# Attention and MLP-mixer on one core: the first k and q by another queue, fewer separate denominators, finer waits

## The chip, the cores and the metric

The kernel runs on one core of one Trainium2 chip. The metric is the device time of one execution in microseconds; of several runs the median is taken. A profile is one execution taken by the hardware profiler; its times are in microseconds from the start of its span.

## What is computed

Eight batches of attention with eight heads of 64 columns over 576 positions, with a decay that depends on a running sum of max(s, 0), and on its output one block of an MLP-mixer:

```python
scores = scale * np.matmul(q, k.transpose(0, 1, 3, 2))
cum = np.cumsum(np.maximum(s, 0.0), axis=-1)
bias = -(cum[:, :, :, None] - cum[:, :, None, :])
scores = np.where(causal, -1000000000.0, scores + np.minimum(bias, 0.0))
attn = np.exp(scores - max); attn = attn / (sum(attn) + 1e-09)
x = heads side by side of np.matmul(attn, v)                 # 8 x 576 x 512
h = np.maximum(xt @ w_tok1, 0.0) @ w_tok2                    # over tokens, 256 wide
u = x + h.transpose(0, 2, 1)
out = u + np.maximum(u @ w_ch1, 0.0) @ w_ch2                 # over channels, 1536 wide
```

## The kernel before

The work is not written in the order in which it runs. Functions (`stage_qk`, `stage_v`, `quad`, `pair`, `tok`, `chan`) hand operations to a planner, `Plan`: each with the engines that may do it, its occupancy and latency on each, what it reads and writes, which buffer it takes and a priority. `Plan.run` walks through time with one clock for each engine and one for the transfers (`dma_free`), always takes the operation that can start first, and among near equals the one of lowest `prio`. The result is one order of instructions for each engine, fixed when the kernel is built. On the chip an engine keeps to that order and waits on semaphores, so an instruction that waits holds up all that stands behind it on its engine. Holes that the plan sees on TensorE in the first 45 us (`WARM`) are filled with products of a zero tile (L1114, "fillers").

Attention goes by batch `b` and by quads of four heads (`h` = 0 and 4). For a quad, k and q are loaded in the layout of 64 rows of 9 x 64 numbers (`load_cast`, L462): by a POOL DMA that casts float32 to bf16 on the way. TensorE transposes the tile (L672), ScalarE or VectorE copies the transposes to kT and qT (L682, L684). A quad holds two pairs, `pair(b, h)` with heads h and h + 2, so that batch 0 has pairs 0, 1, 4 and 5. A pair's scores are computed in two pieces into the two banks of the ring psc (L714); in batch 0 two products first preset the bank with the mask neg (L705), which VectorE builds (L531, L535) from `keep` (POOL, masks.py) and a zeroed tile (ScalarE, L526). ScalarE takes the exponential of a piece of 1024 columns into E (L722).

The decay is folded into v: s is summed along the positions on VectorE (L515, L517, L520), ScalarE takes exp of it into wn (L523), TensorE transposes that (L543), VectorE copies it to wT (L547) and multiplies it into v (`merge_v`, L614). vp has a column more than v, which holds the weight itself (`ones`, L623), so that the product of E and vp gives the denominator in column D. In batch 0 the pairs with h < 5 (0, 1 and 4, `apart`) compute denominators apart: 18 products of one column (L766) into a tile bd as soon as the column is there, and one reciprocal for both heads (L772); their attention products (L784) then leave the column out. These three pairs use banks of the ring pmx, pair 5 one of psc. VectorE or ScalarE normalises into x (L796, L802).

`tok(b)` does the product over tokens (L877 first), and `chan(b)` that over channels: the first product into g in 12 blocks of 128 channels (L995), copied out with max(., 0) (L1002, L1004), and the second product (L1021) in three steps of four blocks (`th`). In the plan, each of the second product's operations reads the whole of g:

```python
gkeys = [(g, cc, a) for cc in range(NCC) for (a, e) in spans]
```

POOL's loads form a chain: each stands after the one before and waits for the eighth before it (`load_op`). The order written at the end of the kernel begins with k and q of quad 0, `ident`, one tile of v, k and q of quad 4, `identf`, `keep`, then the rest of v and the weights. SyncE loads s (L504) and the last tile of v (L592), and later the results.

Of the kernel before, what the change touches and what calls it, by code (L numbers as in the profile page):

```python
# [8 lines left out]
FP32 = mybir.dt.float32  # L9
# [45 lines left out]
class Plan:  # L55
# [50 lines left out]
    def run(self, eps=0.03):  # L106
# [11 lines left out]
        for o in ops:  # L118
            if o.nd == 0:
                for e in o.alts:  # L120
                    cands[e].append(o)
        dma_free = 4.5
        mode = 0
# [19 lines left out]
        while left:  # L143
# [32 lines left out]
            e, est, o = best  # L176
# [191 lines left out]
def kernel(  # L368
# [12 lines left out]
    nc = tc.nc  # L381
# [78 lines left out]
    def load_cast(n, b, h, i, src):  # L460
        def load():
            nc.gpsimd.dma_start(  # L462
                out=n.t[:, i, :, :],
                in_=src[b, h : h + 4, :, :].rearrange("(f e) (p r) d -> (e p) f (r d)", e=2, r=R))
        load_op(load, [(n, i)], 1.6 if i and not (b or h) else 1.45, prio=-1 if b or h else -3)

# [36 lines left out]
    neg = sb("neg", [128, 2, 512], BF16, fast)  # L503
    nc.sync.dma_start(out=s_sb[:, :], in_=s.rearrange("b h s -> (b h) s"))  # L504
    nc.vector.memset(one_sb[:, :], 1.0)
# [7 lines left out]

    P.op({"SP": (0.6, 2.95, lambda: None)}, writes=["s"], prio=-1)
    P.op(dve(576, lambda: nc.vector.tensor_scalar_max(out=s_sb[:, :], in0=s_sb[:, :], scalar1=0.0)),  # L515
# [66 lines left out]
    def stage_v(b, cs=tuple(range(NJ))):  # L582
        if b not in vbuf:
            vbuf[b] = Buf(r_vf), Buf(r_vp[b % 2])
        vf, vp = vbuf[b]
        odd = b % 2
        for c in cs:
            n = min(128, S - c * 128)
            p0 = 64 if odd and n < 128 else 0

            def load_first(c=c, n=n, p0=p0):
                nc.sync.dma_start(out=vf.t[p0 : p0 + n, c, :, :],  # L592
                                  in_=v[b, :, c * 128 : c * 128 + n, :].rearrange("h p d -> p h d"))

            def load(c=c, n=n, p0=p0):
                nc.gpsimd.dma_start(out=vf.t[p0 : p0 + n, c, :, :],  # L596
                                  in_=v[b, :, c * 128 : c * 128 + n, :].rearrange("h p d -> p h d"))
            if b == 0 and c == NJ - 1:
                P.op({"SP": (0.6, 4.6, load_first)}, writes=[(vf, c)], prio=-2)
                continue  # L600
            load_op(load, [(vf, c)], 1.15 * n / 128, 0.92)
        if b:
            merge_v(b, cs)

    def merge_v(b, cs=tuple(range(NJ))):
# [16 lines left out]
        def ones(eng):  # L622
# [3 lines left out]
        P.op({"POOL": (0.5, 0.7, lambda: ones(nc.gpsimd))} if b else {"DVE": (0.25, 0.3, lambda: ones(nc.vector))},  # L626
             reads=["wT"], writes=[(vp, "w")], prio=b * 10 + 5 if b else -1, lock=True)

# [26 lines left out]
    def quad(b, h):  # L655
# [4 lines left out]
        for ti in range(2):  # L660
# [6 lines left out]
            def tr(ti=ti, pv=pv):  # L667
                for r in range(R):
                    for e in range(2):
                        p0 = e * PR  # L670
                        for f in range(2):
                            nc.tensor.transpose(out=pv(e)[f * D : f * D + D, r * PR : (r + 1) * PR],  # L672
                                                in_=nat.t[p0 : p0 + PR, ti, f, r * D : (r + 1) * D],
                                                identity=ident[p0 : p0 + PR, p0 : p0 + PR])
            P.op({"PE": (R * 0.031, R * 0.031 + 0.21, tr)}, reads=[(nat, ti), "ident"] + pads,
                 writes=[(pts[e], e) for e in range(2)], holds=[d[ti] for d in dsts], prio=(np_ - 30 * (b < 1 and h < 1), 2), mode=1)
# [13 lines left out]
    def pair(b, h, kT, qT):  # L690
# [66 lines left out]

        if apart:
            for hh in range(2):
# [14 lines left out]
            P.op({"DVE": (0.2, 0.25, rcp0)}, reads=[(bd, 2 * h), (bd, 2 * h + 1)], writes=[(rc, 0), (rc, 1)], prio=-4)  # L774
        DE = D if apart else D + 1

# [12 lines left out]
        if b == 0:  # L789
            if not apart:  # L790
                def rcp1():
                    nc.vector.reciprocal(out=rc.t[:, :, :], in_=pav2()[:, :, :, D])
                P.op({"DVE": (0.25, 0.3, rcp1)}, reads=[(pas[0], 0), (pas[1], 1)], writes=[(rc, 0), (rc, 1)], prio=-4)
            for hh in range(2):
                def nrm(hh=hh):
                    nc.vector.tensor_tensor(  # L796
                        out=x.t[:, :, (h + 2 * hh) * D : (h + 2 * hh) * D + D], in0=pav(hh)[:, :, 0:D],
                        in1=rc.t[:, hh, :].unsqueeze(2).to_broadcast([128, NJ, D]), op=ALU.mult)
# [181 lines left out]
    def chan(b, u, us, uT):  # L980
# [4 lines left out]
        for (cc, (a, e)) in ([(cc, sp) for hf in range(2) for sp in spans for cc in range(6 * hf, 6 * hf + 6)] if b < 2 else  # L985
                             [(cc, sp) for cc in range(NCC) for sp in spans]):
            if True:
# [5 lines left out]
                def mm(cc=cc, pm=pm, a=a, e=e):  # L993
                    for m in range(NMC):
# [11 lines left out]
                     reads=[(pm, 0)], writes=[(g, cc, a)], prio=0)  # L1006
        gkeys = [(g, cc, a) for cc in range(NCC) for (a, e) in spans]
        for ci, c in enumerate((4, 0, 1, 2, 3) if odd else (0, 1, 2, 3)):
# [7 lines left out]
            for (na, ne) in ([(0, DM)] if whole else [(0, DM // 2), (DM // 2, DM)]):  # L1016
                pm = Buf(r_mx, False)
                for th in range(3):
                    def mm(c=c, pm=pm, th=th, na=na, ne=ne):
                        for cc in range(th * 4, th * 4 + 4):  # L1020
# [18 lines left out]

    stage_qk(0, 0)  # L1040

    def pool_first(occ, fn, key):
        P.op({"POOL": (occ, occ + 0.1, fn)}, writes=[key], prio=-2, after=chain[-1])
# [119 lines left out]
```

## Time and profile before

| | |
|---|---|
| median of 3 runs | 304.81 us (303.45 to 305.19) |
| profiled execution | 303.32 us, its span 301.6 us |
| TensorE busy | 291.0 us, 96% of the span |
| ScalarE, VectorE, POOL busy | 182.5, 174.2, 108.8 us |
| granted TensorE clock, mean | 0.997 |

Rows in order of time give the start, the duration, the engine, the line, the operation with its tiles (out<-in), how many instructions are merged in the row, and in square brackets the idle time before it and what ended it. PE is TensorE, PEld its loading of weights, ACT ScalarE, DVE VectorE, POOL GpSimd, SP SyncE; SPq is SyncE issuing a transfer. Rows of a table by stretches give the stretch, its length, the busy time of PE, PEld, DVE, ACT and POOL, the clock, the share of the transfer engines and GB/s. Rows of transfers give the issuing line, the count, the size of each and the time from issue to landing. TensorE's rows can overlap by some tenths, since its products are pipelined.

### The profile page before, as it was taken

Reading aid. Unit: us, or ns where it says so; the run is one execution under the profiler, and the core shown is the slowest. Engines: PE = TensorE matmul, PEld = TensorE weight load, DVE = VectorE, ACT = ScalarE, POOL = GpSimd, SP = SyncE. Lnnn points to the kernel's source line nnn. Section 1 sums busy time; section 2 is a strip of 40 time slices with the busy share of each in tenths; the row PEclk is TensorE's granted clock in tenths of the full one; section 3 lists DMA queues with packets and bytes.
Section 4 is the critical chain, followed back from the end, with each engine's and each line's share of the span. In section 5 each row is a group of like instructions: output and inputs, shape, how many; then the busy total and the mean of one; then the engine's idle time right before and its main releaser. Section 6 shows DMA issues by size and latency. Waiting matters only on the chain.

```text
span 301.6 us, 8120 instructions
## 1 busy us (share of the span) xinstructions
PE 291.0 (96%) x3431; PEld 169.1 (56%) x3467; DVE 174.2 (58%) x365; ACT 182.5 (61%) x298; POOL 108.8 (36%) x146
## 2 busy tenths in 40 slices
PE   8899999999999999999999999999999999999993
PEld 3468566557754545446764555456764544447542
DVE  6671799597786547665646638776546543430022
ACT  4897994697894587627873277756770367107500
POOL 8885477999491246307440105800000000000000
PEclk9999999999999999999999999999999999999998
DMA  7999999999995593557753461993003310161032
GB/s 133 232 206 206 209 231 232 233 201 282 164 201 103 142 221 59 104 119 149 164 80 73 137 117 23 169 152 125 2 3 70 113 65 0 52 125 51 4 105 77
DMA packets 38348, 38.70 MB, mean 128 GB/s; under 512 B 17600, under 2 KB 31488, under 8 KB 38304
## 3 DMA queue, kind: packets, MB, share of 16 engines
q0 software_dynamic: 17616, 24.84, 45.8%
q1 hardware_dynamic: 20688, 13.26, 16.4%
q8 instruction: 29, 0.48, 0.6%
q14 instruction: 15, 0.12, 0.1%
HBM read 40.65 MB, written 9.44 MB: 166 GB/s over the span
## 4 chain that ended last, share of the span: by engine, by line
PE 83%; DMA 10%; DVE 2%; POOL 2%; issue 2%; ACT 1%; POOLq 0%
PE pmx L995 30%; PE pmx L1021 30%; DMA wc<-in_moe_w_ch_dram 7%; PE pmx L877 5%; PE psc L784 5%; PE psc L714 5%; PE pmx L939 4%; PE psc L672 3%; DMA vf<-in_v_dram 2%; POOL qkn L462 1%; DVE E L739 1%; ACT E L722 1%; POOL vf L596 1%; DVE E L731 0%; DVE ub L946 0%
## 5 line engine op out<-in xcount | busy, mean ns | idle before, releaser
L722 ACT ACTIVATE E<-psc 128x1024 bf16<-128x1024 f32 x64 | 62.1, 1024 | 24.2 <-PE psc L714 23.9
L995 PEld LDWEIGHTS <-wc 128*128 128x128 bf16 x624 | 57.9, 98 | 31.0 <-issue 0.4
L995 PE MATMUL pmx<-uTb,wc 128*128 128x320 bf16 (+2 forms) x384 | 55.9, 299 | 0.0
L1021 PE MATMUL pmx<-wc,gb 128*128 128x512 bf16 (+1 forms) x242 | 54.0, 369 | 0.8 <-issue 0.5
L995 PE MATMUL pmx<-uTa,wc 128*128 128x512 bf16 (+1 forms) x232 | 44.4, 336 | 0.5
L1021 PE MATMUL pmx<-wc,ga 128*128 128x512 bf16 x185 | 43.2, 379 | 0.4
L614 POOL TENSOR_TENSOR vp<-vf,wT 128x512 bf16<-128x512 f32 (+1 forms) x31 | 32.9, 1077 | 26.8 <-PE psc L784 26.1
L630 ACT ACTIVATE junk<-qkn 128x1152 bf16<-128x1152 bf16 x32 | 37.3, 1167 | 7.0 <-DMA qkn<-in_q_dram 6.6
L1002 ACT ACTIVATE gb<-pmx 128x320 bf16<-128x320 f32 (+2 forms) x58 | 25.2, 436 | 20.8 <-PE pmx L995 17.1
L1021 PEld LDWEIGHTS <-gb 128*128 128x128 bf16 x252 | 23.4, 98 | 24.4
L596 POOL DMA_DIRECT2D vf<-in_v_dram x39 | 33.5, 873 | 5.8 <-DMA wc<-in_moe_w_ch_dram 4.0
L731 DVE TENSOR_TENSOR E<-E,keep 128x512 bf16<-128x512 bf16 x56 | 25.8, 470 | 13.0 <-ACT E L722 12.9
L462 POOL DMA_DIRECT2D qkn<-in_k_dram x20 | 14.9, 744 | 46.9 <-issue 44.0
L1021 PEld LDWEIGHTS <-ga 128*128 128x128 bf16 x192 | 18.3, 98 | 20.5
L1002 ACT ACTIVATE ga<-pmx 128x512 bf16<-128x512 f32 (+1 forms) x39 | 20.3, 522 | 11.1 <-PE pmx L995 10.4
L784 PEld LDWEIGHTS <-E 128*128 128x128 bf16 x576 | 21.2, 97 | 6.4 <-DVE E L739 0.6
L1004 DVE TENSOR_SCALAR gb<-pmx 128x320 bf16<-128x320 f32 (+2 forms) x38 | 18.3, 489 | 10.8 <-PE pmx L995 10.7
L813 DVE TENSOR_TENSOR x<-psc,rc 128x640 bf16<-128x640 f32 x28 | 23.1, 824 | 0.9
L682 ACT COPY kT<-psc 128x576 bf16<-128x576 bf16 x18 | 10.6, 642 | 21.3 <-PE psc L672 21.2
L1029 DVE TENSOR_TENSOR of<-pmx,ua 128x512 f32<-128x512 f32 x16 | 11.1, 691 | 20.8 <-PE pmx L1021 18.8
L714 PE MATMUL psc<-qT,kT 64*128 64x256 bf16 (+2 forms) x320 | 21.3, 250 | 0.3 <-DVE qT L684 0.2
L784 PE MATMUL psc<-vp,E 128*128 128x65 bf16 x522 | 20.7, 193 | 0.5 <-DVE E L739 0.5
(100 smaller groups left out, 297.7 us busy)
## 6 DMA issues: line engine op xcount, KB each, us to landing
vf<-in_v_dram POOLq DMA_DIRECT2D x32, 256.0 KB, 7.1
out_dram<-of SPq DMA_DIRECT2D x31, 256.0 KB, 2.4
qkn<-in_k_dram POOLq DMA_DIRECT2D x20, 288.0 KB, 6.2
qkn<-in_q_dram POOLq DMA_DIRECT2D x20, 288.0 KB, 7.7
wc<-in_moe_w_ch_dram POOLq DMA_DIRECT2D x8, 384.0 KB, 10.4
out_dram<-of SPq DMA_DIRECT2D x10, 128.0 KB, 2.5
vf<-in_v_dram POOLq DMA_DIRECT2D x7, 128.0 KB, 7.5
w<-in_moe_w_tok_dram POOLq DMA_DIRECT2D x2, 256.0 KB, 7.3
```

The costliest lines, as they stand in the source:

```text
L596: nc.gpsimd.dma_start(out=vf.t[p0 : p0 + n, c, :, :], in_=v[b, :, c * 128 : c * 128 + n, :].rearrange("h p d -> p h d"))
L614: eng.tensor_tensor(out=vp.t[p0 : p0 + n, c, :, 0:D], in0=vf.t[p0 : p0 + n, c, :, :], in1=wT[p0 : p0 + n, cw, b * H : b * H + H].unsqueeze ...
L630: nc.scalar.activation(out=junk[:, :].rearrange("p (t n) -> p t n", t=2), in_=i, func=AF.Square, accum_out=sq[:, col : col + 1])
L714: nc.tensor.matmul(out=ps.t[:, hh * 512 + c0 : hh * 512 + c0 + e - a], lhsT=kT.t[hh * 64 : hh * 64 + 64, j0 : j0 + 128], rhs=qT.t[hh * 64 ...
L722: nc.scalar.activation(out=E.t[:, :, 512 * pc : 512 * pc + 512], in_=ps.t[:, :].rearrange("p (e n) -> p e n", e=2), func=AF.Exp, scale=0.125)
L731: nc.vector.tensor_tensor(out=o, in0=o, in1=keep[:, :].unsqueeze(1).unsqueeze(1).to_broadcast([128, 2, 2, 128]), op=ALU.mult)
L784: nc.tensor.matmul(out=o[:, ic, 0:DE], lhsT=E.t[:, hh, d0 : d0 + 128], rhs=vp.t[:, jc, h + 2 * hh, 0:DE], start=(jc == j_lo), stop=(jc == ic))
L813: nc.vector.tensor_tensor(out=x.t[:, :, :].rearrange("p c (g f e d) -> p g e f c d", f=2, e=2, d=D)[:, h // 4, h % 2], in0=pav2()[:, :, :, ...
L995: nc.tensor.matmul(out=pm.t[:, 0 : e - a], lhsT=wc1[:, m, cc * 128 : cc * 128 + 128], rhs=uT.t[:, m, a:e], start=(m == 0), stop=(m == NMC ...
L1002: lambda cc=cc, pm=pm, a=a, e=e: nc.scalar.activation(out=g.t[:, cc, a:e], in_=pm.t[:, 0 : e - a], func=AF.Relu),
L1004: lambda cc=cc, pm=pm, a=a, e=e: nc.vector.tensor_scalar_max(out=g.t[:, cc, a:e], in0=pm.t[:, 0 : e - a], scalar1=0.0)),
L1021: nc.tensor.matmul(out=pm.t[:, na:ne], lhsT=g.t[:, cc, c * 128 : c * 128 + 128], rhs=wc2[:, cc, na:ne], start=(cc == 0), stop=(cc == NCC - 1))
```

## The change

- k and q of batch 0's quad 0 are loaded by SyncE as float32 into a stretch of g's second buffer (`gb`), which is not used until much later; four copies, one for each tensor and pair of heads (f), cast them into the same bf16 tile as before; either ScalarE or VectorE can do each. SyncE's order is now k, q, s, last tile of v.
- POOL begins with `ident` and `keep`; then come k and q of quad 4, `identf`, the four tiles of v.
- Only pair 0 (`early`) still has denominators apart. Pairs 1 and 4 take the 65th column and a reciprocal for each head.
- A step of the second channel product reads only the four blocks of g that it uses.
- Some of the planner's costs, due times and priorities are changed.

In the built order, the presets of neg for the first two score banks come before k's transposes, and one filler stands between; eight fillers stand between k's and q's transposes; k's transposes of quad 4 come before the first scores. ScalarE and VectorE each cast one half of k and one of q. VectorE, not ScalarE, copies all of quad 4's kT and qT in batch 0, wn's exponential stands between the first two exponentials of scores, and all 72 attention products of batch 0 stand behind its last scores. No filler is left after the start of `tok(0)`.

```diff
-        dma_free = 4.5
+        dma_free = 6.0
...
-        load_op(load, [(n, i)], 1.6 if i and not (b or h) else 1.45, prio=-1 if b or h else -3)
+        load_op(load, [(n, i)], 1.45, prio=-1 if b or h else -3)
...
-    nc.sync.dma_start(out=s_sb[:, :], in_=s.rearrange("b h s -> (b h) s"))
...
-    P.op({"SP": (0.6, 2.95, lambda: None)}, writes=["s"], prio=-1)
+    first = Buf(r_qn)
+    stage = r_gb.tiles[0][:, :, :].rearrange("p c n -> p (c n)").bitcast(FP32)
+    stage = stage[:, 0 : 4 * R * D].rearrange("p (t f n) -> p t f n", t=2, f=2)
+    for ti, src in enumerate((k, q)):
+        def load0(ti=ti, src=src):
+            nc.sync.dma_start(out=stage[:, ti, :, :],
+                              in_=src[0, 0:4, :, :].rearrange("(f e) (p r) d -> (e p) f (r d)", e=2, r=R))
+        P.op({"SP": (0.6, 4.0 + 0.9 * ti, load0)}, writes=[("stage", ti)], prio=-9 + ti)
+        for f in range(2):
+            def cast0(eng, ti=ti, f=f):
+                if eng:
+                    nc.vector.tensor_copy(out=first.t[:, ti, f, :], in_=stage[:, ti, f, :])
+                else:
+                    nc.scalar.copy(out=first.t[:, ti, f, :], in_=stage[:, ti, f, :])
+            P.op({"ACT": (*c_act(576), lambda cast0=cast0: cast0(0)),
+                  "DVE": (0.1 + 576 * 0.00104, 0.25 + 576 * 0.00104, lambda cast0=cast0: cast0(1))},
+                 reads=[("stage", ti)], writes=[(first, ti, f)], prio=-6)
+    P.op({"SP": (0.6, 4.8, lambda: nc.sync.dma_start(out=s_sb[:, :], in_=s.rearrange("b h s -> (b h) s")))},
+         writes=["s"], prio=-7)
...
-                P.op({"SP": (0.6, 4.6, load_first)}, writes=[(vf, c)], prio=-2)
+                P.op({"SP": (0.6, 5.5, load_first)}, writes=[(vf, c)], prio=-2)
...
-             reads=["wT"], writes=[(vp, "w")], prio=b * 10 + 5 if b else -1, lock=True)
+             reads=["wT"], writes=[(vp, "w")], prio=b * 10 + 5 if b else -5, lock=True)
...
-        if apart:
+        early = b == 0 and h < 1
+        if early:
             for hh in range(2):
                 def den(hh=hh):
...
-        DE = D if apart else D + 1
+        DE = D if early else D + 1
...
+                def rcp2(hh=hh):
+                    nc.vector.reciprocal(out=rc.t[:, hh, :], in_=pav(hh)[:, :, D])
+                if apart and not early:
+                    P.op({"DVE": (0.2, 0.25, rcp2)}, reads=[(pas[hh], hh)], writes=[(rc, hh)], prio=-4, alone=pas[hh])
...
-        gkeys = [(g, cc, a) for cc in range(NCC) for (a, e) in spans]
...
-                         reads=gkeys + [("wc2", i) for i in range(th * 4 // 3, (th * 4 + 3) // 3 + 1)],
+                         reads=[(g, cc, a) for cc in range(th * 4, th * 4 + 4) for (a, e) in spans] + [("wc2", i) for i in range(th * 4 // 3, (th * 4 + 3) // 3 + 1)],
...
-    stage_qk(0, 0)
+    qkn[(0, 0)] = first
...
     pool_first(0.55, lambda: make_identity(nc, ident), "ident")
-    stage_v(0, (0,))
+    pool_first(0.6, lambda: make_upper_triangular(nc, keep, val=1.0, diag=True), "keep")
     stage_qk(0, 4)
     pool_first(0.95, lambda: make_identity(nc, identf), "identf")
-    pool_first(0.6, lambda: make_upper_triangular(nc, keep, val=1.0, diag=True), "keep")
+    stage_v(0, (0,))
```

More of the change, by code (lines that the diff above doesn't have):

```diff
@@ L674, in tr @@
                                                 identity=ident[p0 : p0 + PR, p0 : p0 + PR])
-            P.op({"PE": (R * 0.031, R * 0.031 + 0.21, tr)}, reads=[(nat, ti), "ident"] + pads,
+            P.op({"PE": (R * 0.031, R * 0.031 + 0.21, tr)}, reads=([(nat, ti, 0), (nat, ti, 1)] if b == 0 and h == 0 else [(nat, ti)]) + ["ident"] + pads,
                  writes=[(pts[e], e) for e in range(2)], holds=[d[ti] for d in dsts], prio=(np_ - 30 * (b < 1 and h < 1), 2), mode=1)
@@ L1038, in chan @@
                 P.op({"SP": (0.6 if c < NJ - 1 else 1.2, 0, st)}, reads=[(o, na)], prio=0, dma=128 * 0.088 / 16)
-    stage_qk(0, 0)
+    qkn[(0, 0)] = first
     def pool_first(occ, fn, key):
-        P.op({"POOL": (occ, occ + 0.1, fn)}, writes=[key], prio=-2, after=chain[-1])
+        P.op({"POOL": (occ, occ + 0.1, fn)}, writes=[key], prio=-2, after=chain[-1] if chain else None)
         chain.append(P.ops[-1])
     pool_first(0.55, lambda: make_identity(nc, ident), "ident")
-    stage_v(0, (0,))
+    pool_first(0.6, lambda: make_upper_triangular(nc, keep, val=1.0, diag=True), "keep")
     stage_qk(0, 4)
     pool_first(0.95, lambda: make_identity(nc, identf), "identf")
-    pool_first(0.6, lambda: make_upper_triangular(nc, keep, val=1.0, diag=True), "keep")
+    stage_v(0, (0,))
     P.op({"DVE": (0.6, 0.7, neg_tri)}, reads=["neg0", "keep"], writes=["neg"], prio=-5)
```

## The prediction

> **What bounds the kernel now.** I read the page first (parts 1, 2 and 4), then the table of busy time by stretches, then the instructions in order of time for the first 24 us, and TensorE alone from 19 to 66 us.
>
> ```profile
> span 301.6 us, 8120 instructions
> PE 291.0 (96%) x3431; PEld 169.1 (56%) x3467; DVE 174.2 (58%) x365; ACT 182.5 (61%) x298; POOL 108.8 (36%) x146
> GB/s 133 232 206 206 209 231 232 233 201 282 164 201 103 142 221 59 104 119 149 164 80 73 137 117 23 169 152 125 2 3 70 113 65 0 52 125 51 4 105 77
> PE 83%; DMA 10%; DVE 2%; POOL 2%; issue 2%; ACT 1%; POOLq 0%
> ```
>
> ```profile
> 120.00:200.00 80.00, 79.37 (x877) 43.63 (x884) 51.04 (x100) 50.51 (x77) 27.70 (x36) 1.00 0.59 114
> 200.00:280.00 80.00, 79.47 (x780) 45.16 (x786) 35.99 (x73) 38.88 (x67) 0.00 (x0) 1.00 0.28 65
> ```
>
> TensorE (first column) is busy 79.4 of every 80 us in the long middle. Nothing in the diff shortens that work, so the change can only pay by what happens before TensorE becomes full, or by a hole it closes. "Busy" before about 21 us is partly filler: products of a zero tile that the program puts into planned holes. The rows of the start (start us, duration, engine, line):
>
> ```profile
> 0.76 0.60 SPq L504 DMA_DIRECT2D s_sb<-in_s_dram  x1
> 1.20 5.83 PE L1114 MATMUL pmx<-zero 128*128 128x512 bf16 x15 [1.20 <-DVE zero L470]
> 1.26 0.84 POOL L462 DMA_DIRECT2D qkn<-in_k_dram  x1 [0.81 <-POOLq L1147]
> 1.60 0.28 DVE L483 MEMSET vp<- 64x264 uint32 x1
> 2.04 1.04 ACT L526 COPY neg<-zero 128x1024 bf16<-128x1024 bf16 x1
> 2.66 0.09 DVE L472 MEMSET kT<- 128x32 uint32 x1
> 2.72 0.17 DVE L474 MEMSET E<- 128x128 bf16 x1
> 2.81 0.22 POOL masks.py:197 MEMSET ident<- 128x128 bf16 x1
> 3.12 0.29 POOL masks.py:199 TENSOR_SCALAR_AFFINE_SELECT ident<-ident 128x128 bf16<-128x128 bf16 x1
> 4.26 0.70 POOL L462 DMA_DIRECT2D qkn<-in_k_dram  x1
> 4.55 1.35 DVE L517 TENSOR_TENSOR_SCAN cum<-one_sb,s_sb 64x576 f32<-64x576 f32 x1
> 4.94 0.73 POOL L462 DMA_DIRECT2D qkn<-in_q_dram  x1
> 5.45 0.15 PEld L1114 LDWEIGHTS <-zero 128*128 128x128 bf16 x1 [0.28 <-issue]
> 5.87 0.15 PEld L1114 LDWEIGHTS <-zero 128*128 128x128 bf16 x1 [0.28 <-issue]
> 6.12 0.78 ACT L523 ACTIVATE wn<-cum,half 64x576 f32<-64x576 f32 x1 [3.02 <-DVE half L520]
> 7.00 0.36 PEld L672 LDWEIGHTS <-qkn 64*64 64x64 bf16 x36 [0.42 <-DMA qkn<-in_k_dram]
> 7.53 0.64 ACT L682 COPY kT<-pmx 128x576 bf16<-128x576 bf16 x1 [0.64 <-PE pmx L672]
> 7.58 0.76 DVE L684 COPY kT<-pmx 128x576 bf16<-128x576 bf16 x1 [1.49 <-PE pmx L672]
> 8.25 0.28 DVE L531 TENSOR_SCALAR neg<-keep 128x512 bf16<-128x512 bf16 x1
> 8.68 0.48 PE L672 MATMUL pmx<-ident,qkn 64*64 64x64 bf16 x36 [0.68 <-DMA qkn<-in_q_dram]
> 10.49 1.94 ACT L722 ACTIVATE E<-psc 128x1024 bf16<-128x1024 f32 x2
> 12.50 0.71 POOL L820 DMA_DIRECT2D wc<-in_moe_w_ch_dram  x1 [0.51 <-DMA qkn<-in_q_dram]
> 16.53 0.59 PE L705 MATMUL psc<-neg,ident 128*128 128x512 bf16 x2
> 17.49 2.15 ACT L722 ACTIVATE E<-psc 128x1024 bf16<-128x1024 f32 x2 [0.25 <-PE psc L714]
> 17.91 0.49 DVE L796 TENSOR_TENSOR x<-pmx,rc 128x320 bf16<-128x320 f32 x1 [0.98 <-PE pmx L784]
> 18.51 0.60 PE L766 MATMUL pmx<-vp,E 128*128 128x1 bf16 x18
> 19.15 0.22 DVE L772 RECIPROCAL rc<-pmx 128x10 f32<-128x10 f32 x1 [0.27 <-PE pmx L766]
> ```
>
> The reader is to see three links. Transposes wait for k until 7.00 and for q until 8.68. The first exponential starts at 10.49, 1.81 after q's transposes. From there ScalarE runs almost without a break to 19.64 (17.49 + 2.15), and TensorE follows it. Behind that:
>
> ```profile
> 21.19 2.72 PE L877 MATMUL pmx<-x,w 128*128 128x256 bf16 x30 [0.20 <-issue]
> 44.53 0.38 PE L1114 MATMUL pmx<-zero 128*128 128x512 bf16 x1
> 44.97 2.75 PE L1021 MATMUL pmx<-wc,ga 128*128 128x512 bf16 x12
> 54.10 0.32 PE L672 MATMUL psc<-ident,qkn 64*64 64x64 bf16 x17 [0.61 <-issue]
> 65.03 0.51 PE L784 MATMUL psc<-vp,E 128*128 128x65 bf16 x11 [0.52 <-DVE E L739]
> ```
>
> From L877 on TensorE is full but for three holes: the filler of 44.53, and the stops of 0.61 and 0.52. So the change is worth the shift of L877's end (23.9) plus what these holes become.
>
> **The loads by SyncE.** k goes out at 0.76, where s went, and q, s and the last tile of v follow at 0.60 each.
>
> ```profile
> s_sb<-in_s_dram SPq DMA_DIRECT2D x1, 144.0 KB, 2.7
> ```
>
> s, 147 kB, took 2.7 us to land; at 133 to 232 GB/s (slices 1 and 2 of the GB/s line) its bytes are 1.1 to 0.6 of that, so 1.6 to 2.1 are fixed. k, 295 kB, then lands at 3.6 to 5.1, q behind it at 4.9 to 7.3; I take the middles, 4.4 and 6.1, and s at 7.
>
> **k's transposes.** Casting a half is not in this trace. Nearest are the 576-column copies, 0.64 on ScalarE and 0.76 on VectorE; as those read PSUM and these SBUF, VectorE may need half as much. So k is cast by 5.2, at the latest 5.9. It does not matter, for the built order puts seven fillers, four presets of neg (L705) and one more filler ahead of these transposes. The fillers are 0.42 apart until past 5.87 (5.45 to 5.87). Seven from 1.20 end at 4.2. The presets need neg: POOL makes ident and keep first (0.22 + 0.29 each, no DMA ahead, done by 2.4), ScalarE's copy ends at 3.08, VectorE's neg (0.28 and a smaller one) at about 3.9, so they do not wait. Four presets and a filler at 0.42 end at 6.3. k's transposes move from 7.0 to 6.25, not to 5.2.
>
> **q's transposes.** On ScalarE and VectorE q's casts are queued behind kT's copies. kT's copy starts 0.53 after the transposes (7.00 to 7.53): 6.78 to 7.42 on ScalarE, to 7.55 on VectorE; the casts of q end at 8.1 and 8.3. TensorE meanwhile runs eight fillers. q's transposes start at 8.35 instead of 8.68. An early q gains nothing; a q later than 7.4 costs one for one. Exponentials then start at 10.16, a gain of 0.33.
>
> Here a rule of the Trainium skill bears on the fillers ("TensorE: Matmul & The Clock Gate", section "What's actually happening"): the array starts at half clock and gets the full one after about 3.4 us of activity, with the moment varying by some 0.5 us as the window runs freely. The trace had the slow spacing for at least 4.7 us. By that figure, an estimate from the page, the array would be fast from 4.6 on and most presets would take half the time; rival C works out what that would give. The trace so far speaks against it.
>
> **What stands ahead of the first scores.** TensorE now has the second quad's k transposes before them. That load leaves POOL after ident, keep and three pads moved there from VectorE (0.09 + 0.17 + 0.28 there, at most double here): issued at 2.4 to 3.4, instead of 4.26. The first k took 5.7 from issue to use (1.26 to 7.00), the second q at most 7.6 (4.94 to 12.50). I take 5.7, since as few loads stand before it: landed at 8.1 to 9.1, in time for 9.2. Two loads fewer pass POOL's queue, so weights come sooner; TensorE does not wait for them, which is worth nothing.
>
> **The exponentials.** Two copies (0.64 each) leave ScalarE for VectorE. But s comes later and VectorE is at q's cast until 8.3, so the scan (1.35), behind a maximum that I put at 0.6 by those copies, ends near 10.3 and wn (0.78) falls between the first two exponentials instead of into an idle 3.02 us. Eight exponentials: 10.16, one of 0.97, wn, two more to 13.9, and five at 1.08 (half of 2.15, as two score banks turn round with a preset of 0.59 each): the last ends at 19.3, a gain of 0.3.
>
> **Fewer denominators.** Two groups of 18 products go, 1.2 us of TensorE by L766's 0.60, but in a stretch that ScalarE paces. In their place rcp2 makes four reciprocals (0.22 each) for two. All 72 attention products now stand behind the last scores. Pair 4 takes pair 0's two banks and so waits for both its normalisations (0.49 each); VectorE has pair 4's reciprocals ahead of pair 1's normalisation.
>
> ```profile
> 19.70 2.16 ACT L802 ACTIVATE x<-pmx,rc 128x64 bf16<-128x64 f32 x10
> ```
>
> The last scores end at 18.2, just ahead of the last exponential. From 18.3, with 18 products at 0.55 to 0.60: pair 0's products to 18.85, its reciprocal and normalisations to 20.0, pair 4's products to 20.3, reciprocals to 20.6, pair 1's normalisation to 21.1; ScalarE's share of pair 1 (five pieces, half of 2.16, after its reciprocal at 20.2) to 21.3. L877's work begins at 21.4 instead of 21.19, its last heads arrive by 22.7, and it ends about where it did: I take a gain of 0.1. Bounds: a gain of 1.5 if that VectorE chain is hidden, a loss of 1.5 from rival D.
>
> **Finer waits.** The filler before the first second-product at 44.53 goes, since blocks 0 to 3 of g no longer wait for 4 to 11: 44.97 - 44.53 = 0.44. Elsewhere TensorE is full and there is no hole to close: nothing. The stops of 0.61 and 0.52 lie in a stretch whose order changes; I take them as they are, with 1.1 gained or 0.5 lost as bounds.
>
> **Sum.** 0.1 + 0.44 = 0.5. The profiled execution took 303.32 (span 301.6), so 302.8 there. The median of the runs is 304.81; the forecast goes by it: 304.3.
>
> **Rivals.** About 0.5%, 1.5 us, is what a measurement can tell from no change.
> - A, the sum: 304.3. For it: the 72-product tail and cold fillers. 0.47.
> - B, the tail is hidden: 0.33, the denominators' 1.2, the 0.44 and half of the two stops, 0.5, all count: 2.5, or 302.3. For it: the denominators of 18.51 stood right ahead of the last attention products. Against: VectorE's order before pair 1's normalisation. 0.25.
> - C, TensorE is at full speed when the presets come: four of them and a filler then take some 1.2 (0.59 for two, by L705's row) instead of 2.1; k's transposes, kT's copies, q's casts and the exponentials come 0.8 sooner than in A (k's cast, at 5.2 to 5.9, just allows it): 303.5. Against: the rows at 5.45 and 5.87. 0.1.
> - D, the scores wait for the second quad's loads: its k lands at 3.4 + 7.6 = 11.0, so scores come at 11.4 and exponentials at 11.8 instead of 10.16; that is 1.6 worse, and its q, next in TensorE's queue, another 0.4. With A's 0.5 back, 1.5 slower: 306.3. It decides from a landing after 9.4. 0.18.
>
> **Numbers.** 304.3; the range reaches to B and D, 302.3 to 306.3. A's own: 303.3 to 305.3. Faster by over 0.5%: B, less its weaker half-gains, plus a part of C and of A's tail, 0.31. Slower: D's worse part and a stop that grows, 0.17. Within: 0.52.
>
> **What would show it.** Right: k's transposes near 6.25 with fillers just ahead; q's near 8.35 behind ScalarE's cast; first exponential at 10.2; wn behind it; L877's counterpart at 21.2 to 21.6; no filler near 44. Wrong: k's transposes with a DMA as releaser; scores held by qkn; L877's counterpart before 20.5 or after 22; new stops over 1 us between 24 and 66.

## Result, and the profile after

| | before | after |
|---|---|---|
| median of 22 runs each | 303.76 us (302.01 to 305.83) | 305.54 us (304.06 to 307.84) |
| ratio after/before | | 1.0063, interval 1.0042 to 1.0084 |
| profiled execution, span | 303.32, 301.6 | 306.06, 304.3 |
| granted TensorE clock | 0.997 | 0.995 |

The changed kernel is slower by 0.63%, about 1.9 us. The forecast was a gain of 0.5 us, to 304.3 from a base of 304.81, the median of three runs; over 22 runs the base is 303.76, from which the same sum gives 303.3.

The page of the changed kernel, its busy times and the shares of its chain of waits:

```profile
span 304.3 us, 8094 instructions
...
PE 291.8 (96%) x3430; PEld 168.2 (55%) x3430; DVE 172.0 (57%) x368; ACT 182.8 (60%) x298; POOL 107.6 (35%) x147
...
PE 84%; DMA 12%; POOL 1%; issue 1%; DVE 0%; POOLq 0%
```

By these totals nothing much has happened: TensorE is busy for 291.8 us instead of 291.0, and transfers have 12% of the chain instead of 10%. The first 24 us of the changed kernel in order of time (start, duration, engine, line, operation):

```profile
4.17 1.10 PE L722 MATMUL psc<-neg,ident 128*128 128x512 bf16 x4
...
5.44 0.48 PE L689 MATMUL pmx<-ident,qkn 64*64 64x64 bf16 x36
7.61 0.48 PE L689 MATMUL pmx<-ident,qkn 64*64 64x64 bf16 x36
9.22 0.48 PE L689 MATMUL pmx<-ident,qkn 64*64 64x64 bf16 x36 [0.81 <-DMA qkn<-in_k_dram]
10.06 1.02 ACT L739 ACTIVATE E<-psc 128x1024 bf16<-128x1024 f32 x1 [0.75 <-PE psc L731]
...
17.63 1.84 PE L802 MATMUL pmx<-vp,E 128*128 128x64 bf16 x54
18.10 0.89 DVE L818 TENSOR_TENSOR x<-pmx,rc 128x320 bf16<-128x320 f32 x2 [0.70 <-PE pmx L802]
18.91 0.80 DVE L814 RECIPROCAL rc<-pmx 128x5 f32<-128x5 f32 x4
19.62 0.45 DVE L818 TENSOR_TENSOR x<-pmx,rc 128x320 bf16<-128x320 f32 x1
20.23 2.72 PE L899 MATMUL pmx<-x,w 128*128 128x256 bf16 x30
```

The reader is to see that the start did become shorter: the product over tokens begins at 20.23 where it began at 21.19 before, a gain of 0.96. It is all lost again, and more. TensorE alone in the changed kernel, from 19 to 70 us and, behind the dots, from 200 to 212:

```profile
35.50 0.48 PE L689 MATMUL psc<-ident,qkn 64*64 64x64 bf16 x36 [0.62 <-DMA qkn<-in_k_dram]
44.27 3.62 PE L1042 MATMUL pmx<-wc,ga 128*128 128x512 bf16 x16
56.08 0.38 PE L899 MATMUL pmx<-x,w 128*128 128x128 bf16 x4 [1.28 <-issue]
...
206.54 0.70 PE L1017 MATMUL pmx<-uTb,wc 128*128 128x320 bf16 x4 [1.06 <-DMA uTb<-ub]
207.57 1.26 PE L1017 MATMUL pmx<-uTb,wc 128*128 128x320 bf16 x8 [0.33 <-DMA uTb<-us]
```

No filler stands before the second channel product at 44.27, as forecast. But there are four stops of 0.62, 1.28, 1.06 and 0.33, 3.29 together, where before had 0.61 and 0.52, 1.13 together. Now the end. Before's last rows first:

```profile
283.49 0.23 PE L1087 MATMUL pmx<-bad,ones 128*1 128x36 f32 x2
283.65 13.15 PE L1021 MATMUL pmx<-wc,gb 128*128 128x512 bf16 x71
283.76 0.18 DVE L1092 TENSOR_REDUCE flagf<-pmx 1x1 f32<-1x36 f32 x1 [12.51 <-PE pmx L1087]
283.97 0.14 DVE L1093 CAST flagi<-flagf 1x1 int32<-1x1 f32 x1
...
296.84 0.42 DVE L1029 TENSOR_TENSOR of<-pmx,ub 128x256 f32<-128x256 f32 x1 [0.88 <-PE pmx L1021]
```

and after's:

```profile
284.42 13.14 PE L1042 MATMUL pmx<-wc,gb 128*128 128x512 bf16 x72
...
297.49 0.23 PE L1108 MATMUL pmx<-bad,ones 128*1 128x36 f32 x2
297.60 0.42 DVE L1050 TENSOR_TENSOR of<-pmx,ub 128x256 f32<-128x256 f32 x1 [0.89 <-PE pmx L1042]
297.94 0.17 DVE L1113 TENSOR_REDUCE flagf<-pmx 1x1 f32<-1x36 f32 x1
298.14 0.14 DVE L1114 CAST flagi<-flagf 1x1 int32<-1x1 f32 x1
```

One small product has changed its place. It belongs to a guard: the kernel collects in `bad` whether the decay of this input left the range in which its way of computing holds. This product sums `bad`, VectorE reduces the sum and casts it (`flagi`), every engine then reads the flag into a register, and a branch at the end of the program goes to a general computation if it isn't zero. The product has the lowest urgency of all (`prio=(100, 0)`), so the planner puts it into the first hole that it sees on TensorE, or last. In before the last batch's second channel product had to wait for all of g, and in the hole that the plan saw there, at 283.49, stood the product. With the finer waits that hole is gone, and the product stands behind everything, at 297.49.

Counted from the end of VectorE's last addition to the end of the span, before took 301.55 - 297.26 = 4.29 and after 304.31 - 298.02 = 6.29: 2.0 more. With the rows above the two profiled executions balance: the product over tokens starts 0.96 sooner; from there to the start of the last instruction of the second channel product (296.53 before, 297.29 after, by the records of the traces) 1.72 are lost, as much as the stops' 3.29 - 1.13 = 2.16 less the filler of 0.44; and the end is 2.00 longer. -0.96 + 1.72 + 2.00 = 2.76, the spans' difference up to rounding. Smaller pieces are not in this sum, such as the flag product's own 0.16, which stood ahead of the last product only before.

### The profile page after: what moved, and what is told of

Same layout as the page of the kernel before. It is cut to its first block, busy times and chain, and to the rows that moved or that the text cites. A ratio compares the mean times of both kernels' runs of the same rounds, so it can differ in the third digit from the quotient of the medians.

```text
span 304.3 us, 8094 instructions
## 1 busy us (share of the span) xinstructions
PE 291.8 (96%) x3430; PEld 168.2 (55%) x3430; DVE 172.0 (57%) x368; ACT 182.8 (60%) x298; POOL 107.6 (35%) x147
## 4 chain that ended last, share of the span: by engine, by line
PE 84%; DMA 12%; POOL 1%; issue 1%; DVE 0%; POOLq 0%
PE pmx L1017 30%; PE pmx L1042 30%; PE pmx L961 5%; PE pmx L899 5%; PE psc L802 5%; PE psc L731 5%; DMA qkn<-in_k_dram 5%; PE psc L689 3%; DMA wc<-in_moe_w_ch_dram 3%; DMA vf<-in_v_dram 2%; DMA uTb<-us 2%; POOL qkn L462 1%; PE pmx L986 0%; DVE of L1050 0%; POOL keep masks.py:66 0%
## 5 line engine op out<-in xcount | busy, mean ns | idle before, releaser
L1042 PE MATMUL pmx<-wc,gb 128*128 128x512 bf16 (+1 forms) x252 | 55.3, 369 | 0.0
L1017 PE MATMUL pmx<-uTa,wc 128*128 128x512 bf16 (+1 forms) x240 | 45.6, 337 | 0.0
L1042 PE MATMUL pmx<-wc,ga 128*128 128x512 bf16 x192 | 44.1, 379 | 0.0
L1024 ACT ACTIVATE ga<-pmx 128x512 bf16<-128x512 f32 (+1 forms) x36 | 19.2, 535 | 11.7 <-PE pmx L1017 11.1
L462 POOL DMA_DIRECT2D qkn<-in_k_dram x19 | 14.1, 744 | 33.5 <-issue 31.8
L699 ACT COPY kT<-psc 128x576 bf16<-128x576 bf16 x22 | 13.1, 641 | 19.4 <-PE psc L689 17.9
L802 PEld LDWEIGHTS <-E 128*128 128x128 bf16 x576 | 21.1, 97 | 5.5
L731 PEld LDWEIGHTS <-kT 64*128 64x128 bf16 x320 | 12.6, 94 | 14.6 <-issue 11.5
```

The costliest lines, as they stand in the source:

```text
L731: nc.tensor.matmul(out=ps.t[:, hh * 512 + c0 : hh * 512 + c0 + e - a], lhsT=kT.t[hh * 64 : hh * 64 + 64, j0 : j0 + 128], rhs=qT.t[hh * 64 ...
L802: nc.tensor.matmul(out=o[:, ic, 0:DE], lhsT=E.t[:, hh, d0 : d0 + 128], rhs=vp.t[:, jc, h + 2 * hh, 0:DE], start=(jc == j_lo), stop=(jc == ic))
L1017: nc.tensor.matmul(out=pm.t[:, 0 : e - a], lhsT=wc1[:, m, cc * 128 : cc * 128 + 128], rhs=uT.t[:, m, a:e], start=(m == 0), stop=(m == NMC ...
L1024: lambda cc=cc, pm=pm, a=a, e=e: nc.scalar.activation(out=g.t[:, cc, a:e], in_=pm.t[:, 0 : e - a], func=AF.Relu),
L1042: nc.tensor.matmul(out=pm.t[:, na:ne], lhsT=g.t[:, cc, c * 128 : c * 128 + 128], rhs=wc2[:, cc, na:ne], start=(cc == 0), stop=(cc == NCC - 1))
```

## Experiments

Every kernel was timed beside before, and a ratio is to the times that before had then. After itself has 1.0063 (1.0042 to 1.0084). The theory on trial, **T**: the flag product's late place costs the 2 us, and the rest of the change about cancels. Its main rival, **M**: the time is lost in the middle of the run (stops, and an order planned anew), and the end is no more than what follows from it.

### The flag product early in the changed kernel

```diff
-         reads=["bad"], writes=[(bf, 0)], prio=(100, 0))
+         reads=["bad"], writes=[(bf, 0)], prio=(36.5, 0))
```

> The changed kernel with one number altered: the flag product (L1108) gets priority 36.5 instead of 100, so that the built order has it between the first and the second channel product of the last batch, as before the change, and no longer behind the last product. Theory T (tail): the changed kernel loses 1.9 us at its end, because the flag, its reduction, its load into the engines' registers and the branch come only after all products; the span's stretch from the end of the last addition to the end of the span is 6.3 there and was 4.3. T expects 1.9 less than the changed kernel: some 303.6, a ratio to the kernel before of 0.997 to 1.003, and a tail near 4.3. Theory M (middle): the loss lies in stops of TensorE between 24 and 210 us and the flag's place is worth nothing: 305.5, a ratio of 1.006.

Measured: 303.27 us, 0.9992 (0.9968 to 1.0016). On TensorE this product is the only thing that moved, and on VectorE its reduction and cast. The last rows, in order of time:

```profile
core 0 of [0], span 302.0 us
...
283.88 0.23 PE L1108 MATMUL pmx<-bad,ones 128*1 128x36 f32 x2
...
284.15 0.18 DVE L1113 TENSOR_REDUCE flagf<-pmx 1x1 f32<-1x36 f32 x1 [12.50 <-PE pmx L1108]
...
297.23 0.42 DVE L1050 TENSOR_TENSOR of<-pmx,ub 128x256 f32<-128x256 f32 x1 [0.89 <-PE pmx L1042]
```

From the end of the last addition to the end of the span it is 302.0 - 297.65 = 4.3 again. The loss is gone, as T expected, and with it all in the time that set the changed kernel apart from before.

### The flag product late in the kernel before

```diff
-         reads=["bad"], writes=[(bf, 0)], prio=(100, 0))
+         reads=["bad"], writes=[(bf, 0)], prio=(100, 0),
+         after=[o for o in P.ops if list(o.alts) == ["PE"]][-1])
```

> The kernel before with one thing altered: the flag product is made to follow the last product over channels. T expects 1.9 us more than before, a ratio of 1.006, and a tail near 6.3 instead of 4.3. M expects no difference, 1.000.

Measured: 305.43 us, 1.0069 (1.0041 to 1.0096). None of the change is in this kernel, and it has the whole loss. Its end, in order of time:

```profile
core 0 of [0], span 303.3 us
...
296.23 0.23 PE L1087 MATMUL pmx<-bad,ones 128*1 128x36 f32 x2
296.34 0.42 DVE L1029 TENSOR_TENSOR of<-pmx,ub 128x256 f32<-128x256 f32 x1 [0.89 <-PE pmx L1021]
...
296.89 0.14 DVE L1094 CAST flagi<-flagf 1x1 int32<-1x1 f32 x1
```

The end takes 303.3 - 296.76 = 6.5. The price of the place is shown in both directions.

### Only the finer waits in the kernel before

```diff
-        gkeys = [(g, cc, a) for cc in range(NCC) for (a, e) in spans]
...
-                         reads=gkeys + [("wc2", i) ...],
+                         reads=[(g, cc, a) for cc in range(th * 4, th * 4 + 4) for (a, e) in spans] + [("wc2", i) ...],
```

> The kernel before with the finer waits of the second channel product alone. In its built order the filler ahead of the second product of batch 0 is gone and the flag product has moved behind the last product. T expects 1.9 lost and 0.44 gained: 1.5 us more, a ratio of 1.005, tail near 6.3. M expects the gain of 0.44 alone: 0.9985.

Measured: 304.79 us, 1.0042 (1.0021 to 1.0064). In this kernel too the flag product comes last, with nothing else of the change in it (its end, in order of time):

```profile
core 0 of [0], span 302.5 us
...
295.65 0.23 PE L1086 MATMUL pmx<-bad,ones 128*1 128x36 f32 x2
295.75 0.42 DVE L1028 TENSOR_TENSOR of<-pmx,ub 128x256 f32<-128x256 f32 x1 [0.88 <-PE pmx L1020]
```

Its last addition ends at 296.17, 1.09 sooner than before's, and the end then takes 6.3 instead of 4.3. So the finer waits alone move the product, and alone make before slower.

### The changed kernel with the old waits

The edit is that of the run above, reversed.

> The changed kernel with the old waits of the second channel product (each step reads all of g), the loads and denominators as changed. The flag product stands between the two products of the last batch again. T expects the tail's 1.9 back and 0.44 lost: 304.1, a ratio to the kernel before of 1.001. M expects 305.9, 1.008.

Measured: 305.26 us, 1.0054 (1.0030 to 1.0078): a miss for T. The flag product is between the two products again and the tail is short (5.0 from the start of the second product's last instruction, where after has 7.0), but the planner wrote another order from batch 0's second channel product on. That last instruction starts at 299.09, 1.80 later than in after (297.29) and 2.17 later than in the run with the flag product early (296.92). Two of its new stops on TensorE are 0.89 at 44.25, where it waits for the copy of a block of g, and, in the stretch from 60 to 150 us:

```profile
90.55 0.62 PE L802 MATMUL psc<-vp,E 128*128 128x65 bf16 x14 [0.88 <-DVE E L748]
```

The run does not tell T from M. It shows that an edit of what waits for what makes the planner write another order, and that kernels with the flag at the same place can differ by some 0.6% (1.0054 here, 0.9992 with the finer waits). The runs below therefore all have the flag product early (`prio=(36.5, 0)`), so that its place is no part of what they compare; in before that setting alone gives the same order as before.

### Finer waits, with the flag product early, in the kernel before

> The kernel before with the finer waits alone, and the flag product put back between the channel products by priority 36.5. The same without the priority gave 1.0042 and a tail of 7.0 from the start of the last product to the end of the span, against 5.0. With 2.0 us of tail back: 302.7, a ratio of 0.996 to 0.999. If finer waits cost something in the body it stays above 1.000.

Measured: 303.51 us, 0.9996 (0.9973 to 1.0019), just above what was expected. No loss, and no gain of 0.44 that could be measured. Against the finer waits alone (1.0042) it prices the place of the flag once more: on TensorE these two kernels differ in the flag product alone.

### Only the fewer denominators, and only the loads

To the kernel before, the first gives `early` and `rcp2`, the second the loads by SyncE with their casts, the order on POOL and the planner's costs; neither has the finer waits. Both were run with the priority that before gives to the 65th column, and again with that of the change:

```diff
-             reads=["wT"], writes=[(vp, "w")], prio=b * 10 + 5 if b else -1, lock=True)
+             reads=["wT"], writes=[(vp, "w")], prio=b * 10 + 5 if b else -5, lock=True)
```

> The kernel before with fewer separate denominators alone (pairs 1 and 4 take the 65th column), flag product between the channel products. If the 1.2 us of products taken out counted on TensorE, 0.996, with token products of batch 0 beginning near 20; by the prediction's step, which has ScalarE pace that stretch, they begin at 21.2 give or take 0.4, and the ratio is 0.999 to 1.002. Theory G allows up to 1.004 where a new order waits more behind it.

> e6_dens with the same priority -5: fewer denominators without the new loads, old waits. e6_dens gave 1.0018 (0.9994 to 1.0043) with token products of batch 0 at 21.02. The column is early in that kernel anyway, so no difference is expected: 1.000 to 1.003, 21.0 give or take 0.3.

> The loads of the change alone (k, q, s by SyncE, casts, POOL's new order, the planner's costs), with the old denominators and the old waits; the flag product has priority 36.5, so it stands between the two channel products of the last batch as before. With the tail settled, two theories remain for the start. Theory P (it passes through): token products of batch 0 begin 0.5 to 1.0 sooner than the 21.2 of before, and as TensorE is full behind them the whole kernel is 0.5 to 1.0 faster, 0.997. Theory G (given back): they begin as much sooner, but the order that the planner then makes of batches 0 and 1 waits longer between 24 and 150 us, so that 0.999 to 1.004 comes out.

> e5_loads with the weights' column (ones) at the changed priority -5, so that it stands ahead of the merges of v on VectorE: loads alone, old denominators and waits, flag product between the channel products. In e5_loads this column came at 16.4, behind all merges, and all denominators piled up from 17.9; token products of batch 0 came at 24.16. If the late column was the cause, they come at 20.3 to 21.5 here and the ratio is 0.998 to 1.003; if the loads need fewer denominators, since three groups still stand behind the last scores, they come at 22 to 23 and the ratio stays at 1.004 to 1.008.

| | priority -1 | priority -5 |
|---|---|---|
| fewer denominators | 304.83, 1.0018 (0.9994 to 1.0043) | 305.09, 1.0042 (1.0014 to 1.0070) |
| loads | 307.61, 1.0101 (1.0065 to 1.0138) | 304.07, 1.0023 (0.9996 to 1.0049) |

Neither part gains anything alone. Only the first expectation held. The fewer denominators at -5 were to be 1.000 to 1.003; the loads at -1 missed both theories; the loads at -5 have the late start of one alternative (22.48) and the time of the other. The loads with the old priority are the slowest kernel of all. From its first 26 us, in order of time:

```profile
16.44 0.23 DVE L640 CAST vp<-wT 128x32 bf16<-128x32 f32 x1
17.87 0.83 PE L784 MATMUL pmx<-vp,E 128*128 128x1 bf16 x27
24.16 2.04 PE L899 MATMUL pmx<-x,w 128*128 128x256 bf16 x17
```

With s loaded behind k and q, the column of weights comes late; at the old priority VectorE writes it at 16.44 (10.33 in before), all denominators pile up at 17.87, and the product over tokens starts at 24.16, 2.97 later than before. The changed priority, which the prediction does not mention, takes 1.68 of that back (the start is then at 22.48) and most of the loss in time.

### All but the fewer denominators

> Loads and finer waits, with the old denominators and the flag product between the channel products. P expects the gains of both to add: 0.994 to 0.996. G expects the loads' gain to be given back by another order of batches 0 and 1: 0.997 to 1.002, with the start of batch 0's token products 0.5 to 1.0 sooner and that of batch 3's transposes not.

> e8_loads_waits with priority -5: everything of the change but the fewer denominators, with the flag product between the channel products. Its difference from e1_flag_early (0.9992, token products of batch 0 at 20.71) is what fewer denominators are worth beside the loads. If they take their 1.2 us of products off the path: token products of batch 0 at 21.5 to 22.5 here, ratio 1.002 to 1.005. If they are worth nothing, as the prediction had it: 20.7 give or take 0.3, 0.998 to 1.001.

Measured: with the old priority 306.15 us, 1.0047 (1.0019 to 1.0074), outside both theories; with that of the change, so that only the denominators are undone, 304.26 us, 1.0032 (1.0012 to 1.0052). The second against the run with the flag product early (0.9992) prices the fewer denominators beside the loads. TensorE in the kernel with only the denominators undone, from 16 us on:

```profile
18.00 0.83 PE L784 MATMUL pmx<-vp,E 128*128 128x1 bf16 x27
19.14 0.36 PE L784 MATMUL pmx<-vp,E 128*128 128x1 bf16 x9 [0.31 <-DVE rc L790]
...
22.51 2.21 PE L899 MATMUL pmx<-x,w 128*128 128x256 bf16 x20
```

These denominators stand behind the last scores and ahead of attention products; in the run with the flag early, which has only pair 0's, the start is at 20.71, with a first exponential at 10.54 where this kernel has 10.43. That is 1.80 at this place, near what was expected if the products taken out count; of it the times show about 0.4%, or 1.2 us, with intervals that overlap by 0.0004.

### The presets behind k's transposes

In the kernel with the flag product early, batch 0's presets are told to come after the first transposes:

```diff
-                     writes=[(ps, 0)], prio=(np_ - 9, 0))
+                     writes=[(ps, 0)], prio=(np_ - 9, 0), after=first_tr[0])
```

> The changed kernel with the flag product between the channel products (priority 36.5) and one more thing: the presets of batch 0 may come only behind k's first transposes. In the built order ten fillers stand ahead of these transposes, the four presets and three fillers between k's and q's; the rest is the order of e1_flag_early. Question: do presets at the slow product rate hold k's transposes, and does a sooner start reach the end. In e1_flag_early's profile the four presets took 1.91 and k's transposes came at 6.44, in the changed kernel's they took 1.10 and these came at 5.44. Here they come at 5.5 whatever the rate, first exponential at 9.8 to 10.1 (10.54 in e1_flag_early), token products of batch 0 at 20.0 to 20.3 (20.71). If that passes through (P), 0.4 to 0.6 less than e1_flag_early, a ratio to before of 0.996 to 0.998; if waits behind take it back (G), 0.998 to 1.001.

Measured: 304.11 us, 1.0014 (0.9990 to 1.0037), which speaks against P and lies a little above G. The start is as was meant, in order of time:

```profile
5.59 0.69 PE L691 MATMUL pmx<-ident,qkn 64*64 64x64 bf16 x36
9.94 1.02 ACT L741 ACTIVATE E<-psc 128x1024 bf16<-128x1024 f32 x1 [0.24 <-PE psc L733]
...
20.11 2.72 PE L901 MATMUL pmx<-x,w 128*128 128x256 bf16 x30
```

The product over tokens comes 0.60 sooner than in the kernel that it was made from (20.71), and the time does not show it. Further on TensorE has these stops, the first in the stretch from 50 to 70 us, the others in that from 190 to 210:

```profile
55.24 0.22 PE L901 MATMUL pmx<-x,w 128*128 128x128 bf16 x1 [1.09 <-issue]
...
205.57 0.70 PE L1019 MATMUL pmx<-uTb,wc 128*128 128x320 bf16 x4 [0.91 <-DMA uTb<-ub]
206.62 1.26 PE L1019 MATMUL pmx<-uTb,wc 128*128 128x320 bf16 x8 [0.35 <-DMA uTb<-us]
```

They are near the changed kernel's stops at 56 and 206. But the run with the flag product early, from which this kernel was made, has stops too (from 24 to 70 us and from 196 to 212):

```profile
55.47 0.38 PE L899 MATMUL pmx<-x,w 128*128 128x128 bf16 x4 [0.89 <-issue]
64.80 0.38 PE L986 MATMUL pmx<-ident,us 128*128 128x128 bf16 x4 [0.97 <-DVE of L1050]
...
206.94 1.26 PE L1017 MATMUL pmx<-uTb,wc 128*128 128x320 bf16 x8 [0.36 <-DMA uTb<-us]
```

Together 2.22, against 2.35 here and 3.29 in after, whose order on TensorE is the same up to the flag. So the stops change from execution to execution. That they take what the start gave is not shown: of the 0.60, 0.3 are left in the spans of these two executions (301.7 and 302.0), and nothing in the times.

## Why the prediction was wrong

**The step that failed** is in "Finer waits": "Elsewhere TensorE is full and there is no hole to close: nothing." The hole was in the last batch, where the flag product passed through it; closing it sent that product behind everything and cost 2.0 us. TensorE lost nothing there, and so neither the table of busy time by stretches nor the chain of waits, both of which were read, could show it. It shows in the last 20 us in order of time, and in the built order of the changed kernel, whose end the prediction did not compare. In the terms of the sum, the flag's place was a term put at nothing; it measured 2.0, where the sum had 0.5 the other way. The mechanism that the prediction offered for the slower side, rival D at the start, is not what made after slow. That 305.54 lies between 302.3 and 306.3 is luck: the slower end of these bounds came from D.

**k's transposes**, 6.25: 5.44 in after's profile and 6.44 in the run with the flag product early, whose start is the same order. The difference is rival C's condition. In the latter, in order of time:

```profile
4.17 1.91 PE L722 MATMUL psc<-neg,ident 128*128 128x512 bf16 x4
...
6.44 0.69 PE L689 MATMUL pmx<-ident,qkn 64*64 64x64 bf16 x36
...
20.71 2.72 PE L899 MATMUL pmx<-x,w 128*128 128x256 bf16 x30
```

The four presets took 1.91 here and 1.10 in after. So TensorE becomes fast at a moment that changes from execution to execution: in after by the second preset, which by the trace's records starts at 4.46, 3.3 us after the first product of all (1.21); in the other run only behind k's transposes, which took 0.69 at 6.44 where the fast ones take 0.48, more than 5.2 us after it. The Trainium skill ("TensorE: Matmul & The Clock Gate", section "What's actually happening") gives a window of about 3.4 us that runs freely, and a moment that varies for that reason. The traces agree that it varies; here it varied by some 2 us or more (fast at 4.46 in after, still slow at 6.44 in the run with the flag early), more than the half microsecond either way that the page states. C was given 0.1 on the strength of one execution's rows. Of the seven profiles in which the presets start at 4.17, four have them in 1.10 to 1.17 and three in 1.91: when TensorE becomes fast is not a property of the kernel.

**q's transposes and the first exponential**, 8.35 and 10.16: 7.61 and 10.06 in after, 8.89 and 10.54 in the run with the flag product early, 10.49 before. The first exponential gains 0.43 where TensorE is fast by the presets and nothing where it is not; the forecast of 0.33 had assumed the slow products and was too high for them.

**What stands ahead of the first scores.** k of quad 4 was to land at 8.1 to 9.1; TensorE waited for it for 0.81, to 9.22. It landed at 9.18, 6.7 after its issue at 2.51, where the prediction took 5.7: behind the late end of its range, and 0.2 ahead of D's condition, a landing after 9.4. In the profile of the loads alone at priority -5 it landed at 9.76 and the first exponential came at 10.64, so D's condition is met in some executions. "Weights come sooner" was wrong: by the trace's transfers the first of `w_ch1` landed at 20.96 (before 20.06), k of batch 1's second quad at 35.46 (33.85), and TensorE did wait for that, 0.62 at 35.50. With the flag early they landed at 20.10 and 34.08, so part of this is the execution's.

**Fewer denominators**, products taken out "in a stretch that ScalarE paces": wrong beside the loads, where they are worth 1.80 at the product over tokens, and nearly right alone, where they are worth 0.2 to 0.4 there (21.02 and 20.82) and nothing in the times. The prediction made two steps of what is one: since s is loaded behind k and q, the 65th column comes late, and denominators can no longer all run between the scores.

**The product over tokens**, 21.4 with "a gain of 0.1": 20.23 in after, 20.71 with the flag early. The walk along VectorE's chain put the end of pair 1's normalisation at 21.1; by the rows it ends at 19.62 + 0.45 = 20.07. The walk started 0.7 late against after (attention products from 18.3, in the trace from 17.63), 0.2 late against the run with the slow presets (18.10). And it put pair 0's reciprocal behind its attention products, though this pair has its denominators apart: in after the reciprocal ran at 17.18, ahead of them, and the first normalisation began 0.47 after the first product. So the chain was shorter than forecast, but not hidden, as case B has it: two fillers (0.55 from 19.85) still stand ahead of the product over tokens, and the gain there is 0.96, or 0.48 where the presets were slow, not B's 0.33 + 1.2. In the time even that does not show.

**The stops** "as they are, with 1.1 gained or 0.5 lost as bounds": 1.13 became 3.29, a loss of 2.16, beyond the bound; with the same order up to the flag they were 2.22 in another execution. Less the 0.96 of the start and the 0.44 of the filler, 0.76 were lost ahead of the end in after's one execution; by the medians of many, the changed kernel with an early flag is level with before.

**How the late flag costs 2 us.** The kept traces have records of the flag's load into a register and of the branch, which the views leave out. TensorE's branch lasts about 4 us wherever it was looked up; the other engines' last under 0.1. At the end SyncE waits for each engine's last signal:

| | last addition ends | TensorE's branch | TensorE's last signal | VectorE's | span ends |
|---|---|---|---|---|---|
| before | 297.26 | 295.29 to 299.21 | 299.27 | 300.44 | 301.55 |
| after, flag early | 297.65 | 295.68 to 299.52 | 299.58 | 300.86 | 301.96 |
| after | 298.02 | 298.92 to 303.17 | 303.22 | 302.53 | 304.31 |
| before, flag late | 296.76 | 297.67 to 302.13 | 302.19 | 301.46 | 303.27 |

With the flag early, TensorE's branch runs beside the last additions and is over before VectorE is done. With the flag late it can begin only behind the cast and the register load, and TensorE's signal is the last. In all four the span ends 1.1 behind the last of these signals. From the end of the last addition to that signal it is 3.18 before and 5.20 in after: the 2.0. VectorE's signal too comes later in after (4.51 instead of 3.18), so without TensorE's branch 1.3 of the 2.0 would be left.

**What stays open.** Why TensorE's branch lasts 4 us. In after, five fetches of instructions fall into it (48 KB between 299.9 and 301.8); that it waits for them is argued from their place, not shown. Nor is it known why VectorE's signal comes 3.0 to 3.8 us behind VectorE's own branch. Also open is why the stops near 55 and 205 us come with the new order. At 206.54 and 207.57 TensorE waits for transposing transfers. The third of `ub` landed at 206.50, 8.7 after its issue, where before it took 5.4, and that of `us` at 207.52, 6.6 after its issue, where before it took 3.9. The issue of the latter held SyncE for 3.72 in after, where the same took 1.55 before; in after, SyncE's rows from 196 to 212:

```profile
200.91 3.72 SPq L977 DMA_TRANSPOSE uTb<-us  x1
```

A load of q by POOL in the same stretch also took longer (10.2, before 7.6). What held them up was not tried.

## What to carry to other kernels

- A loosened wait can cost time without any engine losing any: with a planner that fills holes, what stood in the closed hole goes somewhere else. Compare the whole built order, its last instructions too, and ask of each that moved who waits for it.
- What the end of the program hangs on (a flag, a register load, a branch) belongs early; here it was worth 0.7% with one number, more than all that the rest of the change did to the time. A view of busy engines does not show such a branch: look at what each engine does behind its last instruction.
- A gain at the start of a kernel whose bounding engine is full is worth what reaches the end. Here 0.5 to 1.0 us at the first 20 us did not show in the times; behind them stood stops of 0.3 to 1.3 us, at 35, 55, 65 and 206, that differ from one execution to the next. The start itself differs by as much: 0.48 of after's 0.96 are gone in the run whose presets were slow.

## What the runs showed of the hardware that was not expected

- The same flag, reduced and cast in 0.3 us, costs 2.0 us more when it is the last thing in the program than when it is computed some 13 us earlier (from the last addition to the end 4.3 in before and in the first run; 6.3 to 6.5 in after and in the second and third). TensorE's branch on it lasted 3.84 to 4.46 us in the four kernels of the table, the other engines' under 0.1.
- Four 512-column products took 1.10 or 1.91 us at the same place of the same order (4.17), depending on the execution.
- The issue of one transposing transfer of the same size held SyncE for 1.55 us in before, 2.05 in the run with the flag early and 3.72 in after.
